# Seventy-five tiny marker loads on the load ring of an attention decode kernel, forward and backward

## The chip, the cores and the metric

The kernel runs on one core of one Trainium2 chip. The metric is the device time of one execution in microseconds, the median over several executions. A run counts as fast when it lies within 1.5% of the fastest run of the same kernel. "Engine" below means two things, so it always has a word before it: the compute engines (PE for matmuls, DVE, ACT and POOL for the rest) and the 16 DMA engines that carry the traffic between the chip's memory (HBM) and the core's own (SBUF).

## The reference

One decode step of attention with a cache, mixed by a gate with a small MLP, and the gradients of everything except `B_x`:

```python
q = (x @ wq)                                    # 32 heads of 128
scores = einsum("bhqd,bhkd->bhqk", q, k_cache) * Dh ** -0.5
o = einsum("bhqk,bhkd->bhqd", softmax(scores), v_cache)
a = o.reshape(...) @ wo
b = mish(x @ w1 + b1) @ w2
g = sigmoid(sum(x * gate_w))
out = g * a + (1 - g) * b                       # and its vjp for grad_out
```

The caches are 32 heads x 4096 x 128 bfloat16, 1 MB for each head's K and V. They are read once, and their gradients, of the same size, are written once. That is 2 MB in and 2 MB out for a head, and with the weights and their gradients about 164 MB in all, against one query row of arithmetic.

## The kernel before

Heads are processed one after the other, in one "period" each. All loads are issued from the sync queue (the load ring), nearly all stores from the gpsimd queue (the store ring). K and V have four buffers each. At the top of period h the loads of head h+3 are issued, as soon as the buffers of head h-1 are free.

```python
KB, VB = 4, 4
def load_k(h):
    if h < H:
        kts[h] = kv_in.tile([P, J, Dh], BF16, name="Kn", tag="Kn", bufs=KB)
        nc.sync.dma_start(kts[h][:], Kv[h])
# load_v: the same with Vn
# ... cut ...
for h in range(H):
    hh, g = h % G, h // G
    if hh == 3:
        load_wo(g + 2)
        if g % 2 == 0:
            load_wq(g // 2 + 1)
    load_k(h + 3)
    load_v(h + 3)
    if h + 3 == H - 1 and f"dw1_{RC - 1}" in done:
        nc.sync.dma_start(dw1_v, w1_sb[:])
    # ... cut: bookkeeping ...
    period(h)        # products, softmax, outer products; issues the stores of dK(h-1) and dV(h)
```

What the source does not show is how completion is told. The trace of the kernel before shows it: for each DMA, the semaphore that it waits for and the one that tells of its landing. The 101 DMAs of the sync and scalar queues use eight semaphores (numbers 100, 102 to 106, 109 and 110), in one unbroken turn from 1.80 us on. After the first eight, each of the other 93 waits, itself or in an instruction just before it, for the semaphore that it will signal. None of the 90 on the sync queue left before the DMA eight places earlier, which used that semaphore last, had landed in full. Five of them, from the trace (us):

| issued | DMA | waits for | signals | the DMA eight places earlier landed in full |
|---|---|---|---|---|
| 14.04 | Kn | 106 | 106 | 11.41 |
| 14.67 | Vn | 109 | 109 | 13.90 |
| 16.41 | w2c | 110 | 110 | 16.39 |
| 18.91 | w2r | 100 | 100 | 18.89 |
| 20.52 | w2c | 102 | 102 | 20.50 |

Where that landing came last, the DMA left 16 to 17 ns after it (six DMAs up to 26 us). The trace has 16 landing records for each K or V load. They are taken here as one for each DMA engine, which is the author's reading: no record has an engine's number. "The rotation" below means these turns. A head uses two turns, or up to four where it also loads weights, so eight places back is usually some heads back and long done (by more than 0.1 us for 81 of the 90).

Of the kernel before, what the change touches and what calls it, by code (L numbers as in the profile page):

```python
# [11 lines left out]
BF16 = mybir.dt.bfloat16  # L12
# [4 lines left out]
def kernel(  # L17
# [24 lines left out]
    nc = tc.nc  # L42
# [43 lines left out]
    const = ctx.enter_context(tc.tile_pool(name="const", bufs=1))  # L86
# [31 lines left out]
# [5 lines that stand above are left out]
    def load_v(h):  # L123
        if h < H:
            vts[h] = kv_in.tile([P, J, Dh], BF16, name="Vn", tag="Vn", bufs=VB)
            nc.sync.dma_start(vts[h][:], Vv[h])

    def load_wq(w):
        if w < H // WG:
            wqs[w] = wts.tile([P, RC, WG * Dh], BF16, name="wq_g", tag="wq_g")  # L130
            nc.sync.dma_start(wqs[w][:], wq_v[:, :, w * WG * Dh:(w + 1) * WG * Dh])

    def load_wo(g):
        if g < NG:
            wos[g] = wts.tile([P, G, D], BF16, name="wo_g", tag="wo_g", bufs=3)
            nc.sync.dma_start(wos[g][:], wo_v[g])
# [102 lines left out]
    for i in range(3):  # L239
        t = const.tile([P, 2, G, 2, 2], BF16, name=f"qd2_{i}")  # L240
        nc.gpsimd.memset(t[:], 0.0)
        qds.append(t)
    junk = const.tile([P, WG * Dh], BF16, name="junk")


    gps = {}
# [2 lines left out]
    def add(name, kind, fn, deps=(), head=0):  # L249
        steps.append((name, kind, fn, tuple(deps), head))  # L250
# [485 lines left out]
    def dwq_make(rc):  # L736
        def f():
            t = dwqt[rc] = kv_in.tile([P, J * Dh], BF16, name="dwq_t", tag="Kn" if rc % 2 == 0 else "Vn", bufs=KB)
            nc.vector.tensor_scalar(t[:, 0:CL], dq_bc[:, 0:CL], x_f[:, rc:rc + 1], None, ALU.mult)
        return f  # L740

    def dwq_store(rc):
        (nc.sync if rc else nc.gpsimd).dma_start(dwq_v[:, rc, 0:CL], dwqt[rc][:, 0:CL])
# [12 lines left out]
# [3 lines that stand above are left out]
            assert g == 0 or f"dwo{g - 1}" in done  # L759
            load_wo(g + 2)  # L760
            if g % 2 == 0:
                assert g == 0 or f"dx{RC - 1}_{g - 1}" in done
                load_wq(g // 2 + 1)
        load_k(h + 3)
        load_v(h + 3)
        if h + 3 == H - 1 and f"dw1_{RC - 1}" in done:
            nc.sync.dma_start(dw1_v, w1_sb[:])
            stored.append(1)
        if hh == 1 and g + 1 < NG:
            rest = steps[:]  # L770
            steps.clear()
            prep_steps(g + 1, h)
            steps.extend(rest)
        if h == H - 3:
            for rc in range(RC):
                add(f"dwq{rc}", "D", dwq_make(rc), (f"dqb{NG - 2}",), h + (rc + 1) // 2)
                add(f"dwqs{rc}", "T", lambda rc=rc: dwq_store(rc), (f"dwq{rc}",), h)
        period(h)
        if hh == G - 1:
            mlp_left = steps[:]  # L780
            steps.clear()
            finish_steps(g)
            steps.extend(mlp_left)
# [78 lines left out]
```

## Time and profile before

| | before |
|---|---|
| time | 403.81 us (403.04 to 404.58, 2 runs) |
| span of the profiled run | 400.6 us |
| DVE, PE busy | 76%, 74% |
| moved | 164.93 MB, mean 412 GB/s |

From the page of the kernel before. The first two rows cut the span into 40 slices: the busy share of the 16 DMA engines in tenths, and what they moved. Then the chain of work that ended last, by engine and by line, and the group of matmuls that transposes K tiles (busy us and mean ns of one, then the time PE sat idle just before them and what ended it).

```profile
DMA  8999999999999999999999999999999999999995
GB/s 288 420 415 397 421 426 417 418 423 422 425 419 424 421 422 419 419 424 422 427 415 426 422 423 419 418 428 422 421 424 423 422 421 417 423 422 416 425 378 232
...
DVE 36%; DMA 34%; PE 17%; issue 5%; ACT 4%; SPq 0%; POOL 0%; ACTq 0%; POOLq 0%
...
L587 PE MATMUL tr<-ident_f,Kn 128*128 128x128 f32 x512 | 82.0, 298 | 9.7 <-DMA Kn<-in_A_k_cache_dram 9.7
```

The DMA engines are never below nine tenths from the second slice to the last but one, at about 420 GB/s. PE waits for a K tile only 9.7 us in all. So the memory traffic sets the time (the DMA share is 1.01 from 20 to 380 us, and it can pass 1 a little in this account): a microsecond in which the DMA engines do nothing is hard to make up.

How the load ring is fed, from the sync queue's timeline of the kernel before (start us, duration us, sequencer, line, the DMA; SPq is the sync queue, L121 the K load, L126 the V load). K and V of head 4 are issued at the top of period 1, and K of head 5 about 10 us later:

```profile
30.17 0.33 SPq L121 DMA_DIRECT2D Kn<-in_A_k_cache_dram  x1
30.54 0.43 SPq L126 DMA_DIRECT2D Vn<-in_A_v_cache_dram  x1
40.02 0.33 SPq L121 DMA_DIRECT2D Kn<-in_A_k_cache_dram  x1
```

That V landed on its first DMA engine at 52.8 us and on its last at 57.6 us, by the trace's records of semaphore updates, 27 us after issue. So one to two heads of loads usually queue behind one another on the ring (the median K load landed 23.1 us after its issue, the median V load 27.5). What the sync queue waits for, longest first:

```profile
SPq L121 <- PE sB L720: 168.3, 20, 17.8
SPq L136 <- DMA out_dram<-wo_g: 58.0, 5, 13.3
...
SPq L136 <- DMA wq_g<-in_A_wq_dram: 3.1, 1, 3.1
```

Columns: what ended the wait, total us, times, longest. Most waits are for PE to free a K buffer. The last line is the rotation at work: that wo_g load (the second) has a fresh buffer, but its semaphore (102) is still held by the wq_g load eight places before, which landed in full at 7.07 us; the wo_g load left at 7.09.

### The profile page before, as it was taken

What the parts mean: (1) busy time and instruction counts of PE and PEld (TensorE: products, weight loads), DVE (VectorE), ACT (ScalarE), POOL (GpSimd) and SP (SyncE); (2) the same over time, 40 slices, a digit from 0 to 9 for tenths busy, and PEclk for the clock granted to TensorE, in tenths of its full rate; (3) what the DMA queues carried; (4) which work ended last, traced back from release to release, by engine and by line L of the source; (5) the groups of instructions that cost most, each with busy time, mean ns of one, the idle gap of its engine ahead of it and who ended that gap; (6) DMA issues with size and microseconds to landing.
All of it is one profiled execution on the core that took longest, in us unless ns stands there. A gap on an engine that the chain in (4) does not pass through costs nothing.

```text
span 400.6 us, 13611 instructions
## 1 busy us (share of the span) xinstructions
PE 296.6 (74%) x5872; PEld 268.1 (67%) x5872; DVE 303.5 (76%) x791; ACT 177.1 (44%) x411; POOL 47.2 (12%) x94
## 2 busy tenths in 40 slices
PE   0688898778888788778885988819887888888200
PEld 0588787668777678668875878718776777777200
DVE  2438766646799999856688799837999997899850
ACT  1355555324554455325543555605545455545000
POOL 0001101021110111211110113101110121111000
PEclk9999999959999999959998899977999999999655
DMA  8999999999999999999999999999999999999995
GB/s 288 420 415 397 421 426 417 418 423 422 425 419 424 421 422 419 419 424 422 427 415 426 422 423 419 418 428 422 421 424 423 422 421 417 423 422 416 425 378 232
DMA packets 28360, 164.93 MB, mean 412 GB/s; under 512 B 3260, under 2 KB 3964, under 8 KB 12556
## 3 DMA queue, kind: packets, MB, share of 16 engines
q1 hardware_dynamic: 17136, 93.41, 56.5%
q0 software_dynamic: 11104, 70.64, 42.3%
q8 instruction: 46, 0.75, 0.7%
q14 instruction: 14, 0.11, 0.1%
q10 hardware_dynamic: 60, 0.01, 0.0%
HBM read 82.03 MB, written 82.03 MB: 410 GB/s over the span
## 4 chain that ended last, share of the span: by engine, by line
DVE 36%; DMA 34%; PE 17%; issue 5%; ACT 4%; SPq 0%; POOL 0%; ACTq 0%; POOLq 0%
DMA Kn<-in_A_k_cache_dram 29%; DVE dK_sb L612 9%; DVE dV_sb L612 8%; PE tr L587 7%; DVE junk L385 4%; DMA out_dram<-wo_g 4%; ACT tT L589 4%; PE sA L667 3%; DVE junk L288 3%; PE sA L596 2%; PE sB L720 2%; DVE junk L537 2%; DMA vec_rows<-in_gate_w_dram 1%; DVE wo_g L374 1%; DVE dj L707 1%
## 5 line engine op out<-in xcount | busy, mean ns | idle before, releaser
L589 ACT COPY tT<-tr 128x512 f32<-128x512 f32 x256 | 142.3, 588 | 133.9 <-PE tr L587 133.1
L596 PEld LDWEIGHTS <-tT 128*128 128x128 bf16 x2048 | 79.8, 98 | 40.1 <-ACT tT L589 34.6
L587 PE MATMUL tr<-ident_f,Kn 128*128 128x128 f32 x512 | 82.0, 298 | 9.7 <-DMA Kn<-in_A_k_cache_dram 9.7
L612 DVE TENSOR_TENSOR dV_sb<-p_bf,qd 128x2048 bf16<-128x2048 bf16 x64 | 78.0, 1218 | 0.2 <-issue 0.2
L612 DVE TENSOR_TENSOR dK_sb<-ds_bf,qd 128x2048 bf16<-128x2048 bf16 x64 | 77.7, 1216 | 0.0
L587 PE MATMUL tr<-ident_f,Vn 128*128 128x128 f32 x512 | 72.5, 277 | 0.0
L587 PEld LDWEIGHTS tr<-ident_f,Kn 128*128 128x128 f32 x512 | 61.2, 152 | 11.2 <-issue 11.2
L596 PE MATMUL sA<-qd,tT 128*128 128x48 bf16 x1024 | 48.8, 187 | 23.7 <-ACT dq_all L725 12.7
L587 PEld LDWEIGHTS tr<-ident_f,Vn 128*128 128x128 f32 x512 | 55.9, 141 | 0.0
L596 PE MATMUL sB<-qd,tT 128*128 128x48 bf16 x1024 | 46.1, 183 | 0.0
L667 PEld LDWEIGHTS <-Vn 128*128 128x128 bf16 x1024 | 30.2, 95 | 10.4 <-issue 10.4
L667 PE MATMUL sA<-e_bf,Vn 128*128 128x48 bf16 x1024 | 30.7, 183 | 7.7 <-DVE zs L687 6.1
L629 POOL DMA_DIRECT2D out_dram<-dK_sb x30 | 17.3, 576 | 138.6 <-DVE rz L689 90.6
L720 PE MATMUL sB<-ds_bf,Kn 128*128 128x48 bf16 x1024 | 32.1, 185 | 1.4 <-DVE ds_bf L709 1.4
L671 DVE TENSOR_REDUCE m<-sA 128x1 f32<-128x32 f32 x32 | 6.1, 189 | 35.2 <-PE sA L596 28.5
L720 PEld LDWEIGHTS <-Kn 128*128 128x128 bf16 x1024 | 29.4, 97 | 1.6 <-issue 1.6
L642 POOL DMA_DIRECT2D out_dram<-dV_sb x26 | 14.1, 544 | 136.8 <-DVE o_all L712 50.0
L288 DVE SCALAR_TENSOR_TENSOR junk<-wo_g,da_bc 128x640 bf16<-128x640 bf16 x32 | 26.3, 821 | 2.6 <-ACT da_bc L229 1.1
L385 DVE SCALAR_TENSOR_TENSOR junk<-wq_g,dq_bc 128x1024 bf16<-128x1024 bf16 (+1 forms) x25 | 25.1, 1005 | 0.2
L707 DVE TENSOR_SCALAR_CACHE_REDUCE dj<-sB,rz 128x128 f32<-128x128 f32 x32 | 11.1, 346 | 9.2 <-PE sB L701 9.2
L691 ACT ACTIVATE p_bf<-e_bf,rz 128x64 bf16<-128x64 bf16 x32 | 11.1, 348 | 13.6 <-DVE rz L689 10.7
L698 DVE SCALAR_TENSOR_TENSOR pj<-sB,e_bf 128x32 f32<-128x32 f32 x32 | 6.1, 190 | 12.5 <-PE sB L596 12.4
(152 smaller groups left out, 275.5 us busy)
## 6 DMA issues: line engine op xcount, KB each, us to landing
Kn<-in_A_k_cache_dram SPq DMA_DIRECT2D x32, 1024.0 KB, 23.1
Vn<-in_A_v_cache_dram SPq DMA_DIRECT2D x32, 1024.0 KB, 27.5
out_dram<-dK_sb POOLq DMA_DIRECT2D x30, 1024.0 KB, 11.7
out_dram<-dV_sb POOLq DMA_DIRECT2D x26, 1024.0 KB, 11.8
wq_g<-in_A_wq_dram SPq DMA_DIRECT2D x4, 1280.0 KB, 23.7
wo_g<-in_A_wo_dram SPq DMA_DIRECT2D x8, 640.0 KB, 16.7
out_dram<-wo_g POOLq DMA_DIRECT2D x7, 640.0 KB, 12.2
out_dram<-dwq_t SPq DMA_DIRECT2D x4, 896.0 KB, 18.3
```

The lines of the kernel that those rows point to most:

```text
L288: nc.vector.scalar_tensor_tensor(junk[:, 0:D], in0=wos[g][:, i, :], scalar=1.0, in1=da_bc[:], op0=ALU.mult, op1=ALU.mult, accum_out=gp["do ...
L385: nc.vector.scalar_tensor_tensor(junk[:, c0:c1], in0=wqs[w][:, rc, c0:c1], scalar=1.0, in1=dq_bc[:, w * WG * Dh + c0:w * WG * Dh + c1], op ...
L587: nc.tensor.transpose(tp[:, t, :], flat[:, k * P:(k + 1) * P], ident_f[:])
L589: nc.scalar.copy(sb[:].rearrange("p a b -> p (a b)"), tp[:].rearrange("p a b -> p (a b)"))
L596: nc.tensor.matmul(out[:, 2 * k:2 * k + W], lhsT=tb[:, t, par, :], rhs=vec[:, par, :].unsqueeze(1).to_broadcast([P, W // 2, 2]), start=(pa ...
L612: nc.vector.tensor_tensor(dst[:, a:b, :].rearrange("p j (a b) -> p j a b", b=2), col[:, a:b, :].unsqueeze(2).to_broadcast([P, n, Dh // 2, 2]),
L629: ring(h).dma_start(dKv[h], st["dK"][:])
L642: ring(h).dma_start(dVv[h], st["dV"][:])
L667: nc.tensor.matmul(O, lhsT=vts[h][:, j, :], rhs=st["e"][:, j:j + 1].to_broadcast([P, W]), start=(j == 0), stop=(j == J - 1))
L691: nc.scalar.activation(p_bf[:], e[:].unsqueeze(2).to_broadcast([P, J, 2]), ACT.Copy, scale=rz[:])
L707: nc.vector.tensor_scalar(dj[:], PT, rz[:], None, ALU.mult, ALU.add, accum_out=dd[:])
L720: nc.tensor.matmul(DQ, lhsT=kts[h][:, j, :], rhs=ds[:, j, 0:1].to_broadcast([P, W]), start=(j == 0), stop=(j == J - 1))
```

## The change

The intent is to measure, not to speed up. The author took it that a load of k rows uses k DMA engines, so that fifteen loads of 15 to 1 rows behind a V load would show, by when each lands, how far each DMA engine has got. They are put on the load ring at five heads.

```diff
     junk = const.tile([P, WG * Dh], BF16, name="junk")
+    mark = const.tile([16, 15 * 32 + 8 * 120], BF16, name="mark")
...
         load_k(h + 3)
         load_v(h + 3)
+        if h in (1, 8, 15, 22, 28):
+            m = 0
+            for k in range(15, 0, -1):
+                nc.sync.dma_start(mark[0:k, m:m + 32 + 8 * k], B_w1[0:k, 0:32 + 8 * k])
+                m += 32 + 8 * k
         if h + 3 == H - 1 and f"dw1_{RC - 1}" in done:
```

Nothing reads `mark`, so the results do not depend on it. "Group" below means the fifteen loads of one head.

## The prediction

> **What bounds the kernel now.** The DMA engines. The page's DMA row is 9 in slices 2 to 39 at about 420 GB/s; the table by stage gives a DMA share of 1.01 from 20 to 380 us. The chain of waits alternates: DMA 34% (K landings 29%), DVE 36%, PE 17%. DVE is busy 76%, so DMA idle is hard to win back.
>
> **What the change adds.** 75 loads of 1 to 15 rows of 80 to 304 bytes; nothing is removed. The trace's packets of 26 bytes took 9 ns, of 256 bytes 18, completion writes 9: about 0.4 us on the most loaded engine per group. [...]
>
> **What it moves: the next K load.** In the compiled program before, DMAs from the sync and scalar queues signal eight semaphores in rotation, and each waits for the one eight places earlier to land in full (the queue's waits: the second wo_g load waits 3.1 us for wq_g). Usually that one is four heads back and done. Fifteen loads fill the rotation. After K(h+3), V(h+3) six marks go at once; the seventh needs K(h+3) landed, the eighth V(h+3), and K(h+4) stands behind all fifteen. So K(h+4) is issued about 5 us after V(h+3)'s last engine lands (eight marks, about 0.6 us apart as at the trace's start), and moves 1.1 to 1.5 us later, into an empty load ring. Before, K(h+4) came 5 to 12 us after V(h+3); now about 32 us at h = 1, 28 at 8, 36 at 15, 29 at 22.
>
> **What is critical of it.** In a gap of about 6.5 us on the slowest engine and 10 on a median one (V's landing records: the median engine 3 to 4 us before the last, the first up to 15), only stores move. The stores queued or issued then (2.5 us of an engine per MB: 8 packets of 309 ns) fill about 5 of 6 us on the slowest engine, 5.5 of 9 to 10 on the median. Estimated idle per group: 0.3 to 2 us (slowest), 3 to 4 (median); at h = 28 under 1, because no K load follows and only the dw1 store is late (338 to about 363 us) beside a deep store queue. Sum 5 to 15 us. Late K tiles stall PE for 2 to 5 us at h = 1 and 15, mostly the same loss seen from compute.
>
> **Predicted: 412 us, range 405.5 to 423** (8 in 10). Faster by over 2%: 0.01; within 2%: 0.47; slower by over 2%: 0.52.
>
> **What would show each step right or wrong.**
> - Sync queue's waits: 15 to 25 us at the mark line for K and V landings, five times. If K(h+4) still comes 10 to 12 us after V(h+3), the rotation step is wrong.
> - Mark packets: under 2 us of an engine in total.
> - Page: dips in the DMA row and GB/s (to 250 to 350) near 60, 135, 227 and 305 us only; the load ring silent about 6 us each time while stores run.
> - PE waiting longer for Kn than 9.7 us; K loads just after a gap landing in under 15 us (23 median before).
> - Busy time of DVE, PE and ACT unchanged.
>
> **What would make it wrong.** The stores filling the gap entirely (within 1%); engines, brought level at each group, losing less later than I count; or late K tiles starving the stores too, so that both rings run dry (over 423).

The 0.4 us for the markers is the estimate from the packet times of the trace before, for a DMA engine that carries one packet of every marker; its completion writes are the packets of 4 bytes there, one for each landing record (1520 on the load ring, for 95 DMAs of 16). The 1.1 to 1.5 us from issue to movement can be read from the first load of that trace: issued at 0.73 us, its first packet at 1.86, 15 packets under way at 2.20. The forecast's rotation is the one in the table above.

## The result, and the profile after

The kernel with the change took 415.31 us (415.28 to 415.35, 2 runs) against 403.81 us. The ratio is 1.0304 (95% interval 1.0266 to 1.0342). Ratios in this document are those of fast runs, and not quite the ratio of the medians quoted beside them (here the medians differ by 11.5 us, and the ratio gives 12.3).

From the page after, the same rows as before (its lines count one further in the code below the new tile):

```profile
span 413.5 us, 13685 instructions
...
DMA  8999999999999899999999899999998999999996
GB/s 295 419 411 402 420 377 313 422 416 420 425 421 422 298 403 420 414 422 421 424 420 420 321 398 426 413 424 424 422 396 298 417 425 421 420 421 416 421 425 276
...
DMA 45%; DVE 24%; PE 19%; ACT 4%; issue 2%; SPq 2%; ACTq 0%
DMA Kn<-in_A_k_cache_dram 33%; DMA mark<-in_B_w_dram 11%; PE tr L588 8%; DVE dV_sb L613 6%; DVE dK_sb L613 6%; ACT tT L590 4%; DVE junk L386 3%; PE sB L721 3%; PE sA L597 3%; PE sA L668 2%; DVE junk L289 2%; DMA vec_rows<-in_gate_w_dram 1%; SPq L770 1%; DVE wo_g L375 1%; DVE dwq_t L740 1%
...
L588 PE MATMUL tr<-ident_f,Kn 128*128 128x128 f32 x512 | 83.6, 302 | 16.5 <-DMA Kn<-in_A_k_cache_dram 16.5
```

There are four dips in the GB/s row (377 313, 298 403, 321 398, 396 298) and nothing else. Against 421 GB/s these eight slices of 10.34 us fall short by 564 GB/s summed, which is 13.9 us at full rate. The span grew by 12.9 us. The end of the run is a little better filled than before (425 276 in the last two slices for 378 232), about 2 us by the same sum. So the dips are, by this sum, the whole loss. The markers now stand in the chain that ended last, with 11%.

The sync queue's timeline of the kernel after, at the first group (15 issues merged into one line):

```profile
29.52 0.33 SPq L121 DMA_DIRECT2D Kn<-in_A_k_cache_dram  x1
29.89 0.43 SPq L126 DMA_DIRECT2D Vn<-in_A_v_cache_dram  x1
32.16 30.08 SPq L770 DMA_DIRECT2D mark<-in_B_w_dram  x15
62.34 0.74 SPq L121 DMA_DIRECT2D Kn<-in_A_k_cache_dram  x1
63.12 0.43 SPq L126 DMA_DIRECT2D Vn<-in_A_v_cache_dram  x1
```

The fifteen issues took 30 us of the queue, and K of head 5 left at 62.34 us in place of 40.02. V of head 4 had landed on its last DMA engine at 58.3 us (the eighth marker, which waits for that, left at 58.33), so from then on the load ring held nothing but markers. And what the queue waits for:

```profile
SPq L121 <- PE sB L721: 82.6, 9, 17.6
SPq L770 <- DMA Vn<-in_A_v_cache_dram: 56.3, 14, 5.1
SPq L770 <- DMA Kn<-in_A_k_cache_dram: 44.5, 11, 4.6
```

L770 is the marker line. It waited about 100 us for K and V tiles to land, which no marker reads. At the first group the eighth marker waited for semaphore 106, which V of head 4 signals: that landed in full at 58.32 us, and the marker left at 58.33. Next, the four stretches from the V landing to the restart, with one from the kernel before on top (columns: stretch, its us, busy us of PE, PEld, DVE, ACT, POOL with instruction counts, granted PE clock, DMA share, GB/s):

```profile
57.00:63.00 6.00, 5.22 (x99) 4.87 (x99) 3.86 (x10) 2.45 (x6) 0.53 (x1) 1.00 1.00 419
58.30:64.00 5.70, 5.17 (x105) 4.97 (x104) 3.57 (x8) 2.99 (x8) 0.53 (x1) 1.00 0.81 280
136.10:142.50 6.40, 4.58 (x98) 4.05 (x95) 6.37 (x17) 3.18 (x7) 1.07 (x2) 1.00 0.86 294
229.50:236.00 6.50, 5.20 (x110) 4.65 (x107) 6.47 (x17) 3.83 (x9) 1.06 (x2) 1.00 0.79 297
309.20:315.00 5.80, 4.96 (x113) 4.25 (x110) 5.33 (x14) 2.78 (x7) 0.96 (x2) 1.00 0.67 239
```

The DMA share falls from 1.00 to 0.67 to 0.86 there. The store ring moved 216 to 268 GB/s of it, the load ring 20 to 36. PE and DVE keep working (PE 5.17 of the first 5.70 us): they have tiles in hand.

I also summed the trace's packet records by microsecond. "Idle" below is the time in which fewer than all 16 DMA engines carried a packet, in full-engine-set microseconds, from 20 to 380 us. Before it is 0.0 us, after 7.4 us. "Long packets" is the time by which packets lasted longer than the median packet of their size, over the whole run: 4.5 us before, 10.9 us after (mean of the 16 DMA engines). The added 6.4 us lie almost all at the four restarts, where an 8192-byte packet takes up to 1.7 us in place of 0.31.

### The profile page after: what moved, and what is told of

The parts are those of the page before. It is cut to its first block, busy times and chain, and to the rows that moved or that the text cites. A ratio compares the mean times of both kernels' runs of the same rounds, so it can differ in the third digit from the quotient of the medians.

```text
span 413.5 us, 13685 instructions
## 1 busy us (share of the span) xinstructions
PE 298.1 (72%) x5872; PEld 269.8 (65%) x5872; DVE 303.4 (73%) x791; ACT 177.1 (43%) x411; POOL 47.0 (11%) x94
## 4 chain that ended last, share of the span: by engine, by line
DMA 45%; DVE 24%; PE 19%; ACT 4%; issue 2%; SPq 2%; ACTq 0%
DMA Kn<-in_A_k_cache_dram 33%; DMA mark<-in_B_w_dram 11%; PE tr L588 8%; DVE dV_sb L613 6%; DVE dK_sb L613 6%; ACT tT L590 4%; DVE junk L386 3%; PE sB L721 3%; PE sA L597 3%; PE sA L668 2%; DVE junk L289 2%; DMA vec_rows<-in_gate_w_dram 1%; SPq L770 1%; DVE wo_g L375 1%; DVE dwq_t L740 1%
## 5 line engine op out<-in xcount | busy, mean ns | idle before, releaser
L588 PE MATMUL tr<-ident_f,Kn 128*128 128x128 f32 x512 | 83.6, 302 | 16.5 <-DMA Kn<-in_A_k_cache_dram 16.5
L588 PEld LDWEIGHTS tr<-ident_f,Kn 128*128 128x128 f32 x512 | 62.3, 154 | 18.1 <-issue 16.9
L668 PEld LDWEIGHTS <-Vn 128*128 128x128 bf16 x1024 | 30.1, 96 | 10.2 <-issue 10.2
L279 PE MATMUL qc_ps<-cols_bf,wq_g 128*128 128x1 bf16 x160 | 5.3, 164 | 18.7 <-DMA wq_g<-in_A_wq_dram 18.7
L279 PEld LDWEIGHTS <-wq_g 128*128 128x128 bf16 x160 | 4.9, 100 | 19.2 <-DMA wq_g<-in_A_wq_dram 19.1
## 6 DMA issues: line engine op xcount, KB each, us to landing
out_dram<-wo_g POOLq DMA_DIRECT2D x7, 640.0 KB, 11.5
```

The costliest lines, as they stand in the source:

```text
L279: nc.tensor.matmul(qc_ps[:, hh:hh + 1], lhsT=wq[:, rc, off + hh * Dh:off + (hh + 1) * Dh], rhs=x_bf[:, rc:rc + 1], start=(rc == 0), stop=( ...
L588: nc.tensor.transpose(tp[:, t, :], flat[:, k * P:(k + 1) * P], ident_f[:])
L668: nc.tensor.matmul(O, lhsT=vts[h][:, j, :], rhs=st["e"][:, j:j + 1].to_broadcast([P, W]), start=(j == 0), stop=(j == J - 1))
```

## The experiments

The theory: the fifteen loads fill the rotation of eight semaphores; the next K load is held until V of head h+3 has landed everywhere and eight more markers have been issued; the load ring runs dry and the DMA engines idle. The rivals: (A) tiny packets hold up the DMA engines; (B) the lateness of the next K tile stalls compute; (C) the markers' issue time on the sync queue, in proportion to their number. Every result below was correct. All runs but the change itself were timed in three rounds; "before" had a median of 402.7 us (one load, six, lots of five, last group) and 402.6 us (the others) in the same rounds.

### One load with the same packets

```diff
-            m = 0
-            for k in range(15, 0, -1):
-                nc.sync.dma_start(mark[0:k, m:m + 32 + 8 * k], B_w1[0:k, 0:32 + 8 * k])
-                m += 32 + 8 * k
+            nc.sync.dma_start(mark[0:120, 0:115], B_w1[0:120, 0:115])
```

> At each of the five heads one load of 120 rows of 230 bytes [...] in place of the fifteen loads: the same 27.6 KB and the same 120 tiny data packets on the same ring, but one place in the rotation of eight semaphores. Rotation theory (the next K load is held until V has landed, and the ring runs dry): nothing holds the next K load, so 403 to 405.5 us, no dip of the DMA row, under 1 us of 16-engine idle from 20 to 380 us. Rival A [...]: the cost stays, 412 to 416.

It took 403.79 us, ratio 1.0031 (1.0016 to 1.0047), as expected. Its page has no dips:

```profile
DMA  8999999999999999999999999999999999999995
GB/s 287 417 416 404 420 422 418 421 420 425 424 422 416 422 412 403 423 421 422 420 422 425 423 423 417 406 422 421 421 423 423 423 422 420 422 418 419 425 377 199
```

Idle was 0.05 us. The same bytes in the same number of tiny data packets on the same ring cost a tenth of the change, so rival A can be at most a tenth. What the remaining 0.3% is was not tried.

### Six loads a group

```diff
-            for k in range(15, 0, -1):
+            for k in range(15, 9, -1):
```

> Only the first six loads of each group (15 to 10 rows). The next K load then waits for K(h+3) alone, so it is still issued about 20 us later than before, but some 4 us before V(h+3) is through, so the ring does not run dry. Rotation theory with the empty ring as the cost: 403 to 406 us, no dip. Rival B (lateness of K itself, stalling compute, is the cost): nearly all of it stays, 411 to 415. Rival A or the sync queue's issue time, in proportion to the number of loads (75 of 120 rows' packets, 6 of 15 issues): 408 to 411.

It took 404.64 us, ratio 1.0051 (1.0034 to 1.0068), as the theory had it. The sync queue's timeline at the first group:

```profile
29.81 0.43 SPq L126 DMA_DIRECT2D Vn<-in_A_v_cache_dram  x1
32.13 17.03 SPq L770 DMA_DIRECT2D mark<-in_B_w_dram  x6
53.84 0.36 SPq L121 DMA_DIRECT2D Kn<-in_A_k_cache_dram  x1
```

K of head 5 is still 14 us later than before (53.84 for 40.02), but V of head 4 was not through until 58.4 us. The ring did not run dry, idle was 0.4 us, and the late issue cost almost nothing. Alone, this is a weak test of rival B: by the landing records that K still landed at 63.1 us, against 61.9 before and 67.8 with the change, so compute hardly saw it late. The run of seven below is the better test. By count, rival C wanted 408 to 411; it missed too.

### All loads, in lots of five

```diff
-        if h in (1, 8, 15, 22, 28):
-            m = 0
-            for k in range(15, 0, -1):
+        lots = {b + i * (2 if b < 28 else 1): (b, i) for b in (1, 8, 15, 22, 28) for i in range(3)}
+        if h in lots:
+            m = sum(32 + 8 * k for k in range(15, 15 - 5 * lots[h][1], -1))
+            for k in range(15 - 5 * lots[h][1], 10 - 5 * lots[h][1], -1):
```

> All 75 loads, with the same rows and bytes, but in lots of five at three heads (h, h+2, h+4; at the end 28, 29, 30). No lot fills the rotation: the next K load waits for a load of two heads earlier, the one after for K(h+3). Rotation theory: 403 to 406 us. Rival A and rival C (the issue time of 75 loads on the sync queue, 15 groups of 5): unchanged at 412 to 416.

It took 407.88 us, ratio 1.0130 (1.0115 to 1.0145): a miss for the theory as I had put it, though the rivals' 412 to 416 missed by more. The trace shows where it went. From the waits of its sync queue and its timeline, and then two stretches by stage:

```profile
SPq L771 <- DMA out_dram<-w_sb: 10.2, 1, 10.2
...
353.44 0.42 SPq L774 DMA_DIRECT2D out_dram<-w_sb  x1
358.59 22.25 SPq L771 DMA_DIRECT2D mark<-in_B_w_dram  x10
380.94 0.37 SPq L643 DMA_DIRECT2D out_dram<-dV_sb  x1
```

```profile
340.00:373.00 33.00, 28.34 (x594) 25.52 (x593) 30.32 (x72) 17.56 (x40) 4.70 (x7) 1.00 1.01 419
373.00:380.00 7.00, 2.23 (x60) 1.87 (x59) 5.79 (x12) 0.54 (x2) 0.00 (x0) 0.70 0.44 179
```

There was no microsecond below a share of 0.95 from 20 to 373 us: the four groups in the middle were free. But I had put the last two lots at heads 29 and 30, behind the long dw1 store (w_sb). One of the markers waited 10.2 us for that store to land, and the last stores of the sync queue, which start with dV at 380.94 us, stood behind the markers. The DMA share fell to 0.44 for 7 us. It is the same trap, set once more by my own placement and seen on a store.

### The last group alone

```diff
-        if h in (1, 8, 15, 22, 28):
+        if h in (28,):
```

> Fifteen loads at head 28 alone. No K load follows; only the dw1 store is issued about 40 us later (379 for 338 us in the change's trace). Rotation theory with the empty ring: the stores keep the engines busy, 403 to 405 us. If each group costs the same fifth (2.3 us): 406 us.

It took 403.40 us, ratio 1.0019 (1.0004 to 1.0034), idle 1.0 us. The fifth group is close to free: no K load stands behind it, and the stores keep the DMA engines busy meanwhile (in the change, a DMA share of 1.02 from 350 to 380 us). So the four others carry the loss, some 3 us each.

### All loads, in lots of five in the middle, all fifteen at head 28

```diff
+        lots = {b + 2 * i: (15 - 5 * i, 10 - 5 * i) for b in (1, 8, 15, 22) for i in range(3)}
+        lots[28] = (15, 0)
+        if h in lots:
+            m = sum(32 + 8 * k for k in range(15, lots[h][0], -1))
+            for k in range(*lots[h], -1):
```

> The 75 loads again in lots of five (h, h+2, h+4) at the first four groups, where the split run's trace showed no idle of the engines from 20 to 373 us, and all fifteen of the last group at head 28, which the last-group run showed to be free. The split run's 3.5 us of idle at 374 to 380 us came from its lots at heads 29 and 30, which held the last stores of the sync queue behind the dw1 store. Rotation theory with the empty ring: 403.5 to 406 us, under 1.5 us of idle from 20 to 380 us. Rivals A (packets) and C (issue time of 75 loads): 407.5 or more, as the split run.

It took 405.31 us, ratio 1.0058 (1.0037 to 1.0080), idle 0.7 us. All 75 loads, packets and issues are there and four fifths of the loss are gone. That leaves rivals A and C at most the remaining 0.6% (interval 0.4 to 0.8%).

### Seven, ten and thirty loads a group

```diff
-            for k in range(15, 0, -1):
+            for k in range(15, 8, -1):               # seven
+            for k in range(15, 5, -1):               # ten
+            for k in 2 * list(range(15, 0, -1)):     # thirty, each half as wide
```

> The first seven loads of each group: the next K load waits for V(h+3) to land and nothing stands between, so it is issued about 0.3 us after the landing, in place of 4 to 4.8 us. Empty-ring theory: most of the loss is in the issue of loads 8 to 15 after the landing; here the slowest engine's ring is dry for about 1.7 us: 405 to 408 us. If the full landing itself is what costs, the length of the issue afterwards not mattering: 412 to 415.

> Ten loads: three more issues after V(h+3) has landed, next K load about 1.3 us after the landing. Empty-ring theory: between the seven and the fifteen, 406.5 to 410 us, with 0.3 to 1 us of idle a group. Rival by number of loads (two thirds of 11.5 us): 411.5.

> Thirty loads a group, each half as wide, so the same bytes, twice the packets and fifteen more issues of about 0.5 us after V(h+3) has landed: next K load 11 to 13 us after the landing. In the added 8 us the stores fill about half: 4 us more idle a group, at four or five groups: 424 to 440 us. Rival by bytes: 415. Rival by packets: 427 too, so this run does not tell that one apart; the one-load run does.

Seven took 407.18 us, ratio 1.0112 (1.0081 to 1.0143), as expected. It also speaks against rival B: in its profiled run PE waited less for K tiles than before (7.6 us for 9.7), and still about 4.5 us were lost.

```profile
L588 PE MATMUL tr<-ident_f,Kn 128*128 128x128 f32 x512 | 83.0, 300 | 7.6 <-DMA Kn<-in_A_k_cache_dram 7.6
```

Ten took 411.19 us, ratio 1.0203 (1.0174 to 1.0231), a little over my range and as the rival by number had it. Thirty took 429.86 us, ratio 1.0675 (1.0651 to 1.0699), as expected. Here is the thirty at its first two groups:

```profile
59.00:72.00 13.00, 7.41 (x165) 6.92 (x163) 7.49 (x21) 4.20 (x10) 1.59 (x3) 0.92 0.56 223
141.50:155.00 13.50, 11.01 (x237) 9.63 (x233) 13.06 (x34) 6.98 (x17) 1.59 (x3) 1.00 0.70 264
```

The dry stretch is twice as long and, at the first, emptier. All doses together (the last four columns are from the one profiled run of each; the gap is from V's last landing to the next K issue at heads 1, 8, 15, 22; "lost" is the ratio less 1, times 403 us):

| loads a group | ratio | lost us | gap us | idle us | long packets us over before | idle + long packets |
|---|---|---|---|---|---|---|
| one of 120 rows | 1.0031 | 1.2 | none | 0.05 | 1.0 | 1.0 |
| 6 | 1.0051 | 2.1 | -4.5, -3.9, -4.8, 0.1 | 0.4 | 2.8 | 3.2 |
| 7 | 1.0112 | 4.5 | 0.1, 0.1, 0.1, 0.7 | 1.1 | 4.6 | 5.6 |
| 10 | 1.0203 | 8.2 | 1.2, 1.5, 1.8, 2.1 | 4.5 | 5.6 | 10.1 |
| 15 (the change) | 1.0304 | 12.3 | 4.0, 4.8, 4.3, 4.6 | 7.4 | 6.4 | 13.9 |
| 30 | 1.0675 | 27.2 | 11.6, 11.9, 12.2, 15.5 | 19.0 | 6.9 | 25.9 |

The sum in the last column follows the loss to within 2 us at every dose. It has two parts. The long packets come to 5.6, 6.4 and 6.9 us at ten, fifteen and thirty loads. That restarting the ring costs a near-constant amount, about 1.6 us a group, is the estimate from these three; no run varied the restart alone, and why the packets last longer was not shown. The idle grows with the gap: from fifteen to thirty, 11.6 us for 33.6 us of added gap, a third. In the two stretches of the thirty above, 223 and 264 GB/s still moved; that this was the stores, as in the gaps of the change, is the author's reading. (At thirty, the fifth group costs too; its dip lies after 380 us and is not in these columns.) That the ten fits a straight line by number is no support for that rival: the six, the lots of five and the thirty don't (by number of loads, 11.5 us for fifteen, the six would lose 4.6 us and the thirty 23 us, and the lots of five would lose as much as the change).

## Why the prediction was right, point by point

- **The rotation.** Right: K(h+4) was issued 32.5, 27.5, 34.6 and 28.9 us after V(h+3) at heads 1, 8, 15, 22; predicted were 32, 28, 36 and 29. The one-load, six and lots-of-five runs show that it is the cause.
- **"Six marks go at once."** Wrong, without effect on the time. After the first few, the markers left one by one, about 5 us apart (the fifth to eighth at 43.9, 48.8, 53.7, 58.3 us at head 1), because the K and V loads of head h+2 had not landed either (at head 1 those of head 3 landed in full at 43.92 and 48.81 us). So the sync queue shows 25 waits of up to 5 us for K and V tiles in place of a few of 15 to 25 us.
- **The gap.** About right: 4.0 to 4.8 us to the K issue (predicted about 5), and 1.0 to 1.4 us more to its first packet at the three groups where K came first (at head 22 a wo_g load stood ahead of it).
- **The idle.** In total inside the predicted 5 to 15 us, but made up otherwise: 1.7 to 2.3 us of idle a group as a mean of the 16 DMA engines, between what I had for the slowest and for the median one, and 1.2 to 1.7 us a group of long packets at the restart, a term that I did not have. The idle alone, 7.4 us, would have made about 411 us, near the 412; the missing term, 6.4 us, is nearly half of the account. That the result still lay inside the range is owed to its width (405.5 to 423), so in part to luck.
- **The packets.** Right: the 600 data packets of the markers took 10.2 us in all and the 600 packets of 4 bytes that came with them 5.4 us, so 0.2 us of a DMA engine a group in the mean of 16. The 0.4 us for the most loaded one stays an estimate: one packet of each of the fifteen sizes (0.23 us by their medians) and fifteen of 4 bytes (9 ns each).
- **The landings and the end.** K loads just after a gap landed in 5.4 to 11.5 us (predicted under 15). The dw1 store left at 379 us, not 363, mainly because the heads before it were already some 13 us late: in the last-group run, where they were not, it left at 363.4. In the change it cost no idle (the DMA share was 1.02 from 350 to 380 us); in the last-group run all of the 1.0 us lies at 354 to 363 us, while this store was held.
- **Compute.** Busy time was unchanged (DVE 303.5 to 303.4 us, PE 296.6 to 298.1). PE's wait for K tiles rose from 9.7 to 16.5 us; that is the loss seen from PE, not a second one, since the DMA idle and the long packets already add up to it, and since the seven lost time with a shorter wait.

What stays open: the 0.3 to 0.6% that even the one load and the lots of five cost, and why the ten's second group idled 2.1 us at a gap of only 1.5 us.

## What to carry to other kernels

In the trace of the change a small DMA takes a turn in the rotation like a large one: 75 of its 176 turns are markers, down to one row of 80 bytes. Where a trace shows such turns, before adding some, count the DMAs between a load and the next one that must not be late, and keep that count below the rotation's length (eight here), by one DMA with more rows (ratio 1.0031 here) or by spreading them over heads (1.0058, for 1.0304). Being late cost little here while the ring still held work (the six, 0.5%); most of the loss starts when the last DMA engine lands, and it grows with everything the queue still has to issue (1.1% for seven loads a group, 3.0% for fifteen, 6.8% for thirty). And a probe can empty what it measures: the last eight markers of each group went out on an already dry ring (in the first four groups, the landing records of those of 4 to 1 rows, the early one left out, lie within 0.2 us for each), while the sixteen landing records of every V load already show the spread for nothing (52.8 to 57.6 us for V of head 4 before), if not which DMA engine is which.

## Other measurements

- **The hold on the next load.** With fifteen markers between, K(h+4) left 27.5 to 34.6 us after V(h+3) at heads 1, 8, 15 and 22, in place of 4.4 to 10.2.
- **Landing records of small loads.** In the trace after, the update records of all eight semaphores add up exactly with k + 1 for each of the 75 markers of k rows: one early record, 0.4 to 1.2 us after the start of the issue at head 1, and k landings. Each K or V load has 16. No run here shows which DMA engines they were.
- **First packets after a dry ring.** Beside the stores, at three restarts, 1.0 to 1.4 us passed from the start of the K load's issue to its first packet, 0.62 to 0.68 us from the end of the issue. The first 8192-byte packets then took up to 1.7 us in place of 0.31; the long packets came to 1.2 to 1.7 us a group.
- **Small packets.** A packet of 304 bytes took 20 ns (15 GB/s), one of 8192 bytes 309 ns (26.5 GB/s). 600 small packets came with 0.3% (0.2 to 0.5%) in the one-load run.
- **Spread of one load's landings.** Before, K of heads 5, 12, 19 and 26 landed over 4.2 to 16.2 us from the first landing record to the last; after the change, just behind a dry stretch, over 0.6 to 2.9 us.
